# State products of a chunked gated recurrence: three products of 32 columns per head become one of 96

## The chip, the cores and the metric

The kernel runs on one core of a Trainium2 chip. The engines that matter are TensorE (PE; its weight loads are shown apart as PEld), VectorE (DVE), ScalarE (ACT), GpSimd (POOL) and SyncE (SP), which issues the DMAs. The metric is the time of one execution on the device in microseconds, as the median of the runs. PE multiplies a stationary operand (`lhsT`, the "weights", at most 128 rows by 128 columns) with a moving one (`rhs`) and writes to PSUM. A weight load and the pass that streams the moving operand are two instructions in the trace. An fp32 product shows as two loads and two passes, a transpose as one of each.

## The reference

A gated linear recurrence with complex decay, for each batch (4), head (8) and channel (48) over 768 steps, and behind it a feed-forward block on 3072 tokens:

```python
for t in range(S):
    new_re = ar * S_re - ai * S_im
    new_im = ar * S_im + ai * S_re
    kv = np.einsum('bhd,bhe->bhde', k[:, :, t], v[:, :, t])
    S_re, S_im = (new_re + kv, new_im)
    y[:, :, t] = np.einsum('bhd,bhde->bhe', q[:, :, t], S_re)
...
a = x @ w1
b = x @ w2
h = a * b @ w3
return (h @ w_out).astype(np.float32)
```

`ar` and `ai` are the gates after their magnitude is limited to 0.999; `x` is `y` with the heads laid side by side (3072 by 384); the hidden width is 1024.

## The kernel before

A batch's 768 steps are cut into two units of 384, so there are 8 units, and each unit into three chunks of 128 steps. `gates(u)` works out the running product of the gates (logarithms, exponentials, scans, sine and cosine, on ACT and DVE) and scales and turns q and k with it. In that scaled frame the decay disappears: the output of a step is a masked sum over earlier steps of its chunk plus q times a state that only grows by sums. `move` brings q and k by DMA into tiles `QL` and `KL` of 96 rows (real and imaginary parts of 48 channels) per head. At a unit's end the state is scaled once with `rho`.

For each chunk PE does four kinds of work.

- `turn(u, c, x)` (L677) transposes the chunk's scaled k, three blocks of 128x128 for each of the real and imaginary part, into a PSUM bank `tp`; ACT copies it to `KT` (L679), which then has 128 steps in its rows and 96 columns beside each other per head.
- `state(u, c)` (L742) multiplies `KT` of a head with that head's v (128 steps by 48) into a bank `kv` of 96 rows by 8 heads by 48. The columns of `KT` go in three groups of 32, one product each, into rows 0 to 31, 32 to 63 and 64 to 95 of the bank. DVE then adds `kv` to the state `T` (L748), or ACT copies it where there is no state yet (L746).
- `scores(u, c, x)` (L691) forms the products of q and k in blocks of 32 keys into the banks `sc`; DVE copies them through a causal mask into `A` (L694).
- `outputs(u, c)` (L725) forms `y` from `A` and v and from `T` and `QL`; ACT copies it to `xT` (L727).

The feed-forward work of unit u-1 fills PE between these pieces of unit u: `ffn_ab` (m, L766: products with w1 and w2, then ACT's copy `a`, L771, and DVE's product `ab`, L772), and the output products (o, L853; p, L817) with `w3o`, a product of the two last weight matrices that is formed at the start (f, L995).

The state update runs 20 times: three times in a batch's first unit, twice in its second, whose last state nobody reads. `pieces(u)` lists the pieces of a unit in order and `unit` puts feed-forward work between them; behind `kv` come m, p, sc or, in the first units, tp. The order on PE is the program's own (`manual_schedule`). On ACT, DVE, POOL and SP a planner sets the order, by its own times and by marks of priority such as those on the add into `T`. `tp`, `kv` and `y` share the two banks of the pool `ps_v`.

In the trace's names a form such as 128*32 is the number of rows and columns of the stationary operand that are in use.

Of the kernel before, what the change touches and what calls it, by code (L numbers as in the profile page):

```python
# [375 lines left out]
def kernel(  # L376
# [36 lines left out]
    nc = tc.nc  # L413
    B, H, D, S = qt.shape
# [18 lines left out]
    SB, LANES = 32, C // 32  # L433
# [83 lines left out]
    def load_v(u):  # L517
        b, h = divmod(u, 2)


        vr = one.tile([P, UC, DM], FP, tag="vr", name="vr")
        nc.sync.dma_start(out=vr, in_=v[b, h * TT:(h + 1) * TT].rearrange("(c p) e -> p c e", p=C))
        g_t[u]["vr"] = vr
# [209 lines left out]
    def state(u, c):  # L733

        KT, V = KT_t.pop((u, c)), g_t[u]["vr"][:, c].rearrange("p (h d) -> p h d", d=D)
        n = u % 2 * UC + c
        T = T_t.get((u // 2, n))
        kv = ps_v.tile([2 * D, H, D], FP, tag="v", name="kv")
        for hd in range(H):
            rows = KT[:, hd].rearrange("p d x f -> p (d x f)")  # L740
            for g in range(0, 2 * D, SB):
                nc.tensor.matmul(out=kv[g:g + SB, hd], lhsT=rows[:, g:g + SB], rhs=V[:, hd], start=True, stop=True)  # L742
        Tn = Tb[(u * UC + c) % 3]
        with tc.high_priority():
            if T is None:
                nc.scalar.copy(out=Tn[:, :, 0:D], in_=kv)  # L746
            else:
                add = nc.vector.tensor_tensor(out=Tn[:, :, 0:D], in0=kv, in1=T[:, :, 0:D], op=OP.add)  # L748
                if (u, c) == (0, 1):

                    tc.add_manual_dep(add.ins, begun[-1].ins.name, ORDER, reason="begun")
        if c == UC - 1:
            rho = L_t[u][1][:, :, TT:TT + 1].to_broadcast([2 * D, H, D])
            nc.vector.tensor_tensor(out=Tn[:, :, 0:D], in0=Tn[:, :, 0:D], in1=rho, op=OP.mult)
        T_t[u // 2, n + 1] = Tn
        if u + 1 < NU and c == UC - 1 - u % 2:
            load_v(u + 1)
# [269 lines left out]
    def pieces(u):  # L1027

        sc = [[lambda c=c, x=x: scores(u, c, x) for x in range(2)] for c in range(UC)]
        tr = [[lambda c=c, x=x: turn(u, c, x) for x in range(2)] for c in range(UC)]  # L1030
        kv = [lambda c=c: state(u, c) for c in range(UC)]
        y = [lambda c=c: outputs(u, c) for c in range(UC)]

        if u % 2:
            return [[tr[0][0]], [tr[0][1]], [tr[1][0], kv[0]], [tr[1][1]], [kv[1]], sc[0], sc[1] + [y[0]], sc[2] + [y[1]],
                    [y[2]]]
        return [[tr[0][0]], [tr[0][1]], [tr[1][0], kv[0]], [tr[1][1]], [tr[2][0], kv[1]], [tr[2][1]], [kv[2]] + sc[0],
                sc[1] + [y[0]], sc[2] + [y[1]], [y[2]]]
# [144 lines left out]
```

## Time and profile before

| | |
|---|---|
| median of 3 runs | 560.96 us (560.75 to 561.29) |
| the profiled execution | 561.29 us, span 559.5 us |
| mean granted clock of PE | 0.988 |
| PE busy | 525.5 us, 5474 passes |
| DVE, ACT busy | 334.8 us, 338.0 us |
| L742, passes of kv | 960, 206 ns each by the trace's modelled ends, side by side |
| L742, weight loads of kv | 960, 110 ns each |
| L748, DVE's add into T | 16, 554 ns each |
| L746, ACT's copy into T | 4, 475 ns each |
| kv's share of the chain that ended last | 2% |

Passes on PE overlap, and their recorded ends are modelled, so lengths of single passes can't be added up: what a group costs is read from the start of its first pass to the start of what follows. A group of the profile counts both passes of a product: 20 states x 8 heads x 3 groups x 2 = 960.

### The profile page before, as it was taken

The page shows a single profiled execution, that of the slowest core. Times are in us where ns is not written, and L with a number is a line of the kernel's source. Part 1 is how long each engine was busy: PE and PEld are TensorE (multiplying, and loading weights), DVE is VectorE, ACT ScalarE, POOL GpSimd, SP SyncE. Part 2 cuts the span into 40 slices and gives each one's busy share as a digit, 9 for nine tenths or more (in the row PEclk, how much of TensorE's full clock was granted, in tenths as well). Part 3 has the DMA queues.
Part 4 walks back from the last instruction along what each step waited for, and adds up shares of the span by engine and source line. Part 5 has one row for each costly group of instructions (what it writes and reads, how often), then busy time and mean ns, then how long its engine had stood idle before and what let it go on. Part 6 is the DMA issues. An engine that isn't in the chain of part 4 may idle for free.

```text
span 559.5 us, 13023 instructions
## 1 busy us (share of the span) xinstructions
PE 525.5 (94%) x5474; PEld 359.1 (64%) x5474; DVE 334.8 (60%) x516; ACT 338.0 (60%) x553; POOL 5.2 (1%) x12
## 2 busy tenths in 40 slices
PE   4698789999999999999999999999999999999995
PEld 2354565567656875569656875687557965696564
DVE  8999398936862457536852677446752797332121
ACT  6989665735564688738782898569964845201100
POOL 3000000000000000000000000000000000000000
PEclk9999989999999999999999999999999999999998
DMA  8997988794556557875685565956674204300001
GB/s 254 349 403 175 276 217 262 205 190 139 114 152 131 136 161 203 206 208 152 178 213 159 174 146 164 242 162 184 170 184 135 74 29 95 80 13 30 0 1 49
DMA packets 73156, 89.71 MB, mean 160 GB/s; under 512 B 31104, under 2 KB 62848, under 8 KB 72320
## 3 DMA queue, kind: packets, MB, share of 16 engines
q1 hardware_dynamic: 73088, 88.79, 58.0%
q8 instruction: 45, 0.74, 0.6%
q14 instruction: 23, 0.19, 0.1%
HBM read 65.14 MB, written 4.72 MB: 125 GB/s over the span
## 4 chain that ended last, share of the span: by engine, by line
PE 53%; DVE 18%; ACT 16%; issue 5%; DMA 4%; SPq 2%; DVEq 0%; ACTq 0%
PE m L766 26%; PE o L853 8%; PE p L817 7%; PE y L725 4%; PE sc L691 4%; ACT gZ L562 3%; ACT re L562 3%; DVE gA L598 3%; DVE gZ L621 2%; PE kv L742 2%; ACT gR L562 2%; PE tp L677 2%; ACT gA L562 2%; ACT low L899 1%; DVE gR L640 1%
## 5 line engine op out<-in xcount | busy, mean ns | idle before, releaser
L766 PE MATMUL m<-xT,w1s 128*128 128x384 f32 x384 | 135.3, 489 | 1.8 <-ACT xT L727 1.8
L766 PE MATMUL m<-xT,w2s 128*128 128x384 f32 x384 | 134.5, 487 | 0.3 <-DVE ab L772 0.3
L766 PEld LDWEIGHTS m<-xT,w2s 128*128 128x128 f32 x384 | 72.8, 190 | 51.8 <-DVE ab L772 1.5
L766 PEld LDWEIGHTS m<-xT,w1s 128*128 128x128 f32 x384 | 71.1, 190 | 47.4 <-ACT xT L727 2.4
L772 DVE TENSOR_TENSOR ab<-m,a 128x384 f32<-128x384 f32 x64 | 35.3, 553 | 81.0 <-PE m L766 74.8
L771 ACT COPY a<-m 128x384 f32<-128x384 f32 x64 | 30.3, 475 | 53.9 <-PE m L766 52.7
L853 PE MATMUL o<-w3o,ab 128*128 128x384 f32 x160 | 54.0, 487 | 0.0
L679 ACT COPY KT<-tp 128x384 f32<-128x384 f32 x40 | 33.7, 853 | 31.1 <-PE tp L677 30.9
L694 DVE COPY_PREDICATED A<-mask,sc 128x512 f32<-128x512 uint8 x48 | 33.2, 730 | 14.6 <-PE sc L691 14.4
L853 PEld LDWEIGHTS o<-w3o,ab 128*128 128x128 f32 x160 | 29.6, 190 | 18.7 <-issue 0.4
L725 PE MATMUL y<-A,V 128*32 128x128 f32 x768 | 40.8, 279 | 0.0
L691 PE MATMUL sc<-QL,KL 96*32 96x64 f32 (+3 forms) x1536 | 33.8, 238 | 6.6 <-DVE A L694 3.0
L691 PEld LDWEIGHTS sc<-QL,KL 96*32 96x32 f32 x1536 | 29.1, 112 | 13.0 <-issue 5.1
L725 PE MATMUL y<-QL,T 96*32 96x128 f32 x640 | 36.6, 280 | 0.4 <-issue 0.4
L995 PE MATMUL f<-wo_s,w3s 128*128 128x384 f32 x96 | 36.6, 528 | 0.0
L725 PEld LDWEIGHTS y<-A,V 128*32 128x32 f32 x768 | 34.7, 112 | 1.4 <-issue 1.4
L748 DVE TENSOR_TENSOR T<-kv,T 96x384 f32<-96x384 f32 x16 | 8.8, 553 | 43.6 <-PE kv L742 43.4
L899 ACT ACTIVATE low<-raw 128x384 uint16<-128x384 uint32 (+4 forms) x28 | 24.9, 900 | 14.0 <-DVE low L895 7.3
L725 PEld LDWEIGHTS y<-QL,T 96*32 96x32 f32 x640 | 32.6, 113 | 0.9 <-issue 0.9
L817 PE MATMUL p<-To,So 128*128 128x192 f32 x168 | 31.6, 335 | 0.0
L995 PEld LDWEIGHTS f<-wo_s,w3s 128*128 128x128 f32 x96 | 20.0, 212 | 14.3 <-issue 4.5
L817 PEld LDWEIGHTS p<-To,So 128*128 128x128 f32 x168 | 27.0, 190 | 3.2 <-issue 3.0
(119 smaller groups left out, 738.8 us busy)
## 6 DMA issues: line engine op xcount, KB each, us to landing
look<-in_w_dram SPq DMA_DIRECT2D x28, 512.0 KB, 4.4
raw<-in_w_dram SPq DMA_DIRECT2D x6, 1024.0 KB, 10.6
raw<-in_w_dram SPq DMA_DIRECT2D x8, 768.0 KB, 9.2
KL<-gR SPq DMA_DIRECT2D x24, 192.5 KB, 3.2
KL<-k SPq DMA_DIRECT2D x24, 192.5 KB, 4.0
re<-in_a_re_dram SPq DMA_DIRECT2D x24, 192.0 KB, 5.7
im<-in_a_im_dram SPq DMA_DIRECT2D x24, 192.0 KB, 3.9
k<-in_k_dram SPq DMA_DIRECT2D x24, 192.0 KB, 4.6
```

The costliest lines, as they stand in the source:

```text
L562: chain(nc.scalar.activation(**kw))
L679: nc.scalar.copy(out=KT_t[u, c][:, :, :, x].rearrange("p h d f -> p f d h"), in_=tp.rearrange("p f (d h) -> p f d h", h=H))
L691: nc.tensor.matmul(out=sc[SB * g:SB * g + SB, j, s0:C], lhsT=KL[:, x * n + j, w][:, s0:s0 + SB], rhs=QL[:, x * n + j, w][:, s0:C], start=T ...
L694: masked[:] = [nc.vector.copy_predicated(out=A[:, x * n:(x + 1) * n], data=sc, mask=mask)]
L725: nc.tensor.matmul(out=o, lhsT=a, rhs=b, start=s0, stop=s1)
L766: nc.tensor.matmul(out=m, lhsT=w[:, j * P // WB, f, j * P % WB:j * P % WB + P], rhs=xT_t[u][:, f], start=(f == 0), stop=(f == KD - 1))
L771: copied[:] = [nc.scalar.copy(out=a, in_=got[0])]
L772: nc.vector.tensor_tensor(out=ab_t[u][:, j], in0=got[1], in1=a, op=OP.mult)
L817: nc.tensor.matmul(out=m[p], lhsT=a[:, f], rhs=b[:, f], start=(f == 0), stop=(f == KH - 1))
L853: nc.tensor.matmul(out=m, lhsT=ab_t[u][:, f, t * P:(t + 1) * P], rhs=w3o[:, f], start=(f == 0), stop=(f == KF - 1))
L899: nc.scalar.activation(out=ends.bitcast(U16)[:, 0::2].rearrange("p (r m) -> p r m", r=r), in_=lo.bitcast(U32), func=AF.Copy, scale=2.0 ** -29)
L995: nc.tensor.matmul(out=sums[j], lhsT=w3_t[f][:, j * P:(j + 1) * P], rhs=w3_t["wo"][:, f], start=(f == 0), stop=(f == KF - 1))
```

## The change

In `state`, the three products of 32 columns per head are replaced with one product of all 96 columns. It reads the same `KT` and v and writes the same place in the same bank; there are 8 products per state instead of 24.

```diff
         kv = ps_v.tile([2 * D, H, D], FP, tag="v", name="kv")
         for hd in range(H):
-            rows = KT[:, hd].rearrange("p d x f -> p (d x f)")
-            for g in range(0, 2 * D, SB):
-                nc.tensor.matmul(out=kv[g:g + SB, hd], lhsT=rows[:, g:g + SB], rhs=V[:, hd], start=True, stop=True)
+            nc.tensor.matmul(out=kv[:, hd], lhsT=KT[:, hd].rearrange("p d x f -> p (d x f)"), rhs=V[:, hd],
+                             start=True, stop=True)
         Tn = Tb[(u * UC + c) % 3]
```

Nothing else differs: pools, order of the pieces, loads and stores are the same.

## The prediction

> **What bounds the kernel now.** I read the page first: the line of TensorE's (PE) busy time, its row in the 40 slices, and the chain of work that ended last. Then, from the trace, PE's waits after the start-up, the timeline and the chain around one state update, and the groups of the tiles that are neighbours of it.
>
> ```profile
> PE 525.5 (94%) x5474; PEld 359.1 (64%) x5474; DVE 334.8 (60%) x516; ACT 338.0 (60%) x553; POOL 5.2 (1%) x12
> ...
> PE   4698789999999999999999999999999999999995
> ...
> PE 53%; DVE 18%; ACT 16%; issue 5%; DMA 4%; SPq 2%; DVEq 0%; ACTq 0%
> ```
>
> PE is busy in every slice after the first seven (some 100 us). A busy matmul row is not yet a bound, so the waits decide; this is all that PE waited for from 80 us on:
>
> ```profile
> PE tp L677 <- DVE gR L640: 3.1, 4, 1.3
> PE m L766 <- ACT xT L727: 1.8, 2, 1.1
> PE sc L691 <- issue: 1.4, 3, 0.8
> PE y L725 <- issue: 0.4, 1, 0.4
> PE m L766 <- DVE ab L772: 0.3, 1, 0.3
> PE sc L691 <- DVE A L694: 0.3, 1, 0.3
> PE tp L677 <- ACT KT L679: 0.2, 1, 0.2
> ```
>
> Some 7.5 us in 480 us. The reader should see that what PE issues there sets the pace, and that nothing in the list is a wait of or for kv. One state update in the timeline of PE and its weight loads (start, length, engine, line):
>
> ```profile
> 173.93 0.49 PE L677 MATMUL tp<-ident,gR 128*128 128x128 f32 x3
> ...
> 174.35 0.75 PEld L742 LDWEIGHTS kv<-vr,KT 128*32 128x32 f32 x48 [0.17 <-issue]
> 174.35 0.88 PE L742 MATMUL kv<-vr,KT 128*32 128x48 f32 x48
> ...
> 175.16 1.59 PEld L766 LDWEIGHTS m<-xT,w1s 128*128 128x128 f32 x6
> 175.16 2.20 PE L766 MATMUL m<-xT,w1s 128*128 128x384 f32 x6
> ```
>
> and the chain in the same place, where the whole burst lies on it:
>
> ```profile
> 174.09 0.33 PE tp L677 x3
> 174.42 0.81 PE kv L742 x48
> 175.23 2.78 PE m L766 x8
> ```
>
> Asked at each of the 20 bursts, the chain holds such a piece of 0.81 at 15 of them, all from 174 us on: six followed by m, six by p, three by sc (at 188.98, 310.24 and 431.75). The three at 58, 62 and 64 us lie under a DMA, ACT and DVE chain, and the two of the second unit, at 121.89 and 126.01, under DMAs. Now the durations in ns (least, median, most):
>
> ```profile
> L742 PEld LDWEIGHTS kv<-vr,KT x960: 106/110/110, 58.4 to 488.5; 128*32 128x32 f32 x192
> L742 PE MATMUL kv<-vr,KT x960: 206/206/231, 58.4 to 488.6; 128*32 128x48 f32 x192
> ...
> L766 PE MATMUL m<-xT,w1s x384: 486/486/590, 84.7 to 536.9; 128*128 128x384 f32 x192
> ...
> L677 PE MATMUL tp<-ident,k x60: 272/273/329, 56.3 to 482.5; 128*128 128x128 f32 x60
> ...
> 175.16 0.30 PEld L766 LDWEIGHTS m<-xT,w1s 128*128 128x128 f32 x2
> ```
>
> The most is each time a first pass behind a change of form, which waits in the open for its weights: 25 ns for kv's 32 columns, 104 for m's 128, 57 for a transpose's 128. The last line, a narrow window, has m's first two loads, 0.19 long each, in 0.30: the second starts 108 ns after the first. So a load for products takes 0.83 ns per column. A stream takes as much: m's six passes start 1.93 us apart, 322 ns per 384 columns; 48 columns come to 40 ns and 2.5 for the pass.
>
> **The change part by part.** *Removed:* per state 24 products of 32 columns, recorded as 48 loads and 48 passes (two per fp32 product). *Added:* 8 products of 96 columns, 16 loads and 16 passes. Values, banks and releases stay.
>
> What a burst costs before, from the end of the last transpose's stream (173.93 + 3 x 0.11 = 174.26) to the place where m streams: a gap of 95 ns to kv's first start; the burst of 16 rounds, three passes beside each other 6 ns apart, rounds 42.5 ns apart, whose last starts 675 ns after the first; 40 ns of stream; a gap of 96; 104 for m's bare load. Sum 1011 ns (the three column groups run truly beside each other, or 48 passes would need 2 us). The gap is that of a change of form: all neighbours of one form in this trace follow at 2 to 3 ns (tp to m, m to o), all changes between 128*128 and 128*32 at 93 to 97.
>
> After it, the passes are of 128 rows and 96 columns. I take them for the neighbours' form, since 96 doesn't fit one 32-column group, so that the two changes go, and the first load, 80 ns, fits beside the last transpose's 107 ns. But each pass needs its own 96 columns: 96 x 0.83 + 1.7 = 81.7 ns, under a stream of only 42.5 ns. m's timeline shows that one load goes ahead and the next starts as its pass starts, so the period is the longer of the two. Then: 15 x 81.7 = 1225 to the last pass's start, and 108 for m's load, which starts with it: 1333 ns. That is **+0.32 us** where m or p follows, twelve times: +3.9 us.
>
> Where sc follows, today's 990, 993 and 1030 ns from the previous stream's end to sc's start become 1225 + 40 + 96 (p to sc, as in 15 other places) + 25 for the bare load = 1386: +0.40, +0.39, +0.36, **+1.15 us** in all. Today's gap there is 180, not 96, since four semaphore instructions of 110 ns each stand in PE's queue behind 96 short ones; behind 32 in a longer time they are early, which is counted in that.
>
> The two bursts of the second unit and the three of the start I cost at nothing: behind them PE waits for KT's copy, or for sc (0.25 to 2.3 us in those places), and the chain is a DMA's or the gates'. If that cover failed they would add up to 5 x 0.4 = 2.0 us. The add into T (DVE, 0.55 us) and the copy into T (ACT, 0.48) start later by the growth; their readers, y of a later chunk and the next state, come over 2 us later, and ps_v's bank is asked for again only behind a product of 2 us. On ACT and DVE those two stand ahead of other work that is queued in order; it gets later as PE does, no more. DMA, SP and POOL issue nothing different, besides 1280 fewer PE instructions to fetch.
>
> Does PE's lateness reach the end? At the last burst of each unit the chain goes on in PE and passes from there to ACT or DVE (PE y at 193.95, ACT xT at 194.90, then the gates until PE's wait at 227.17). So the gates are started by PE, and the 3.1 us that PE waits for them don't swallow it.
>
> Sum: 3.9 + 1.15 = +5.0 us. The profiled execution took 561.29 (span 559.5 and 1.8 around it), so 566.3; it is 0.33 above the median of the three, so the median to expect is **566.0**.
>
> The unknown is a load of 96 columns, which no row has. Bounds: it costs as a transpose's does, 57 x 96/128 = 43 ns, and then the stream sets 42.5 to 43: a burst is 15 x 42.5 + 108 = 745, -0.27 x 12, and 798 to sc, -0.20 x 3, **-3.8 us**. Above, it takes the time of 128 columns, 108: 1728, +0.72 x 12, and 1781, +0.78 x 3, **+10.9**. Or 96 columns are a form of their own, with both gaps and both bare loads: 95 + 80 + 1225 + 40 + 95 + 108 = 1643, +0.63 x 12, and +0.56 x 3, **+9.3**. I take 81.7, as 32 and 128 columns of these same two-pass products lie on one line.
>
> The Trainium skill, "TensorE: Matmul & The Clock Gate", section "Part 3: Packing small matmuls — row/col tiling", says that a weight load overlaps a running matmul only where the row groups differ. By that rule a pass here would cost load and stream, 124 ns, and a sum worked out from it would be some +16 us (577). The row speaks against it: m's passes use all 128 rows and still follow at 322 ns, the stream alone.
>
> **The rivals.** *Loads hidden, faster:* the load is no longer than the stream. For it: the transposes' 57 ns per 128 columns. Against: those are one-pass transposes, and m's and p's first passes pay 104. It decides where a pass takes under 60 ns (15 x 60 + 108 = 1008); its time is 560.96 - 3.8 = 557.2. *Dearer loads or a form of its own:* for it, that 96 is in no row; against, the line through 25 and 104. 570.3 to 571.9. *Swallowed by waits:* PE's waits for gR and xT, 4.9 us, shrink by what kv grows: 561 to 563. Against it, the chain comes from PE behind every burst. *Planner:* ACT, DVE and SP are put in order by a planner that works with its own times, and 640 fewer passes may turn neighbours there. One gate step moved past a copy is worth about an operation of 1.2 to 1.4 us per unit, either way: 562 to 570.
>
> **How the numbers follow.** The forecast's case has 0.70 (564.5 to 567.5), hidden loads 0.09, dearer ones 0.08, swallowed 0.04, planner 0.09. Leaving out hidden loads, the part of the swallowed below 562.5 and the dearest gives 562.5 to 570.5, and some 0.85 inside. Faster by over 0.2% (about what a measurement here tells from none): 0.09 and some of the planner's, 0.11; within: 0.03; slower: 0.86.
>
> **What would show it.** Right: 320 passes of kv, starting some 82 ns apart, a burst of about 1.3 us in the chain, no 95 ns gap on either side, and m's first pass recorded 42 ns behind kv's last, some 552 ns long (486 and what its load outlasts kv's stream) instead of 590. Wrong: passes 42 ns apart, gaps of 95 that stay, or PE's waits for gR shrinking by what the bursts grow.

## The result and the profile after

The changed kernel takes 566.66 us (median of 4 runs, 565.88 to 567.67) where the kernel before took 561.12 beside it: a ratio of 1.0097, 95% interval 1.0075 to 1.0119. It is slower by 5.5 us; 566.0 was forecast, with 562.5 to 570.5 as the range.

The page of the changed kernel: PE's line, its chain, and the new group of state products.

```profile
PE 532.0 (94%) x4834; PEld 369.8 (65%) x4834; DVE 334.5 (59%) x516; ACT 337.6 (60%) x553; POOL 5.3 (1%) x12
...
PE 61%; ACT 15%; DVE 14%; DMA 4%; issue 4%; SPq 1%; DVEq 0%; ACTq 0%
PE m L765 27%; PE o L852 9%; PE p L816 9%; PE y L725 5%; PE kv L740 4%; PE sc L691 4%; ACT re L562 3%; DVE gZ L621 3%; PE tp L677 2%; ACT gZ L562 2%; DVE gA L598 2%; DMA look<-in_w_dram 2%; ACT gR L562 2%; ACT gA L562 1%; DVE gR L640 1%
...
L740 PE MATMUL kv<-vr,KT 128*96 128x48 f32 x320 | 29.7, 246 | 1.1 <-ACT KT L679 1.1
```

PE has 640 passes fewer and is busy 6.5 us longer. kv's share of the chain went from 2% to 4%. The rest of the program is as before: DVE and ACT do the same work in the same time.

The timeline of PE and its loads around the state update that the prediction showed (start, length):

```profile
173.53 0.49 PE L677 MATMUL tp<-ident,gR 128*128 128x128 f32 x3
...
173.75 1.46 PEld L740 LDWEIGHTS kv<-vr,KT 128*96 128x96 f32 x16
...
173.85 1.48 PE L740 MATMUL kv<-vr,KT 128*96 128x48 f32 x16
...
175.13 1.59 PEld L765 LDWEIGHTS m<-xT,w1s 128*128 128x128 f32 x6
175.17 2.17 PE L765 MATMUL m<-xT,w1s 128*128 128x384 f32 x6
```

The first load starts at 173.75, under the last transpose, and the first pass directly behind that transpose (173.53 + 3 x 0.11 = 173.86): the gap of 95 ns is gone on both sides. But from the first stream at 173.85 to the moment m's load can begin, at 175.13, the 16 passes take 1.275 us, 15 periods of 85.0 ns. The chain in the same place:

```profile
173.69 0.33 PE tp L677 x3
174.02 1.32 PE kv L740 x16
175.33 2.97 PE m L765 x9
```

The piece that was 0.81 us of 48 passes is 1.32 of 16. And PE's waits from 80 us on:

```profile
PE tp L677 <- DVE gR L640: 3.1, 4, 1.4
PE m L765 <- ACT xT L727: 1.8, 2, 1.0
PE y L725 <- issue: 1.1, 1, 1.1
PE m L765 <- DVE ab L771: 1.0, 2, 0.8
PE m L765 <- ACT a L770: 0.4, 1, 0.4
PE sc L691 <- DVE A L694: 0.3, 1, 0.3
```

The waits for gR and for xT are what they were (3.1 and 1.8 us): they swallowed nothing. The waits called "issue" went from 1.8 to 1.1 us, those for ab and a from 0.3 to 1.4.

With each of PE's other 4514 passes set against its twin in the trace of before, the lateness is -0.4 us ahead of the first burst of the third unit, grows by 0.38 to 0.42 at each of the fifteen bursts from there on, and is +5.2 at the last product. Between the bursts it moves too, and that nearly evens out: +0.8 us between the bursts at 246 and 296 us, where PE now waits 1.0 us for ab instead of 0.3, and -1.2 between those at 310 and 357, most of it where the waits "issue" at 315.0 and 319.8 are gone. The span has grown by 6.4; the other 1.2 us lies behind the last DVE add (5.5 us before, 6.7 after), and with times of 565.9 to 567.7 in four runs I don't lay it to the change.

### The profile page after: what moved, and what is told of

Same layout as the page of the kernel before. It is cut to its first block, busy times and chain, and to the rows that moved or that the text cites. A ratio compares the mean times of both kernels' runs of the same rounds, so it can differ in the third digit from the quotient of the medians.

```text
span 565.9 us, 11743 instructions
## 1 busy us (share of the span) xinstructions
PE 532.0 (94%) x4834; PEld 369.8 (65%) x4834; DVE 334.5 (59%) x516; ACT 337.6 (60%) x553; POOL 5.3 (1%) x12
## 4 chain that ended last, share of the span: by engine, by line
PE 61%; ACT 15%; DVE 14%; DMA 4%; issue 4%; SPq 1%; DVEq 0%; ACTq 0%
PE m L765 27%; PE o L852 9%; PE p L816 9%; PE y L725 5%; PE kv L740 4%; PE sc L691 4%; ACT re L562 3%; DVE gZ L621 3%; PE tp L677 2%; ACT gZ L562 2%; DVE gA L598 2%; DMA look<-in_w_dram 2%; ACT gR L562 2%; ACT gA L562 1%; DVE gR L640 1%
## 5 line engine op out<-in xcount | busy, mean ns | idle before, releaser
L725 PE MATMUL y<-A,V 128*32 128x128 f32 x768 | 39.0, 273 | 0.0
L725 PE MATMUL y<-QL,T 96*32 96x128 f32 x640 | 34.9, 272 | 1.1 <-issue 1.1
L725 PEld LDWEIGHTS y<-A,V 128*32 128x32 f32 x768 | 33.4, 109 | 1.4 <-issue 1.4
L725 PEld LDWEIGHTS y<-QL,T 96*32 96x32 f32 x640 | 31.4, 109 | 1.4 <-issue 1.4
L740 PEld LDWEIGHTS kv<-vr,KT 128*96 128x96 f32 x320 | 29.6, 165 | 2.5 <-ACT KT L679 1.3
L740 PE MATMUL kv<-vr,KT 128*96 128x48 f32 x320 | 29.7, 246 | 1.1 <-ACT KT L679 1.1
```

Source lines behind the costliest of these rows:

```text
L725: nc.tensor.matmul(out=o, lhsT=a, rhs=b, start=s0, stop=s1)
L740: nc.tensor.matmul(out=kv[:, hd], lhsT=KT[:, hd].rearrange("p d x f -> p (d x f)"), rhs=V[:, hd], start=True, stop=True)
```

## The experiments

**Does the load or the stream set the pace?** First, the changed kernel with twice the stream. The second half of what a product writes is written over by the next head's own.

```diff
-            nc.tensor.matmul(out=kv[:, hd], lhsT=KT[:, hd].rearrange("p d x f -> p (d x f)"), rhs=V[:, hd],
+            n2 = min(hd + 2, H)
+            nc.tensor.matmul(out=kv[:, hd:n2], lhsT=KT[:, hd].rearrange("p d x f -> p (d x f)"), rhs=V[:, hd:n2],
```

> The changed kernel, but each product streams the v of two heads (96 columns instead of 48; the second half is written over by the next head's own product, the last head keeps 48). Theory (the load of 96 columns sets the pace, one load ahead): a pass is 85.0 ns in the trace of the changed kernel, the longer stream is 80 + 2.5 = 82.5 ns and fits under it, so passes stay 85 ns apart and the time stays 566.7 us (565.5 to 568). Rival (load and stream of a pass come one after another, since all use the same rows): 14 of 16 passes grow by 40 ns, 0.56 us per state, 15 states on the chain: +8.4, 575 us.

Measured: 568.06 us, ratio to the kernel before 1.0103 (1.0074 to 1.0132), where the changed kernel has 1.0097. The group of kv in its trace, and a burst:

```profile
L741 PE MATMUL kv<-vr,KT x320: 208/248/323, 59.1 to 494.1; 128*96 128x96 f32 x140, 128*96 128x48 f32 x20
...
174.81 1.46 PEld L741 LDWEIGHTS kv<-vr,KT 128*96 128x96 f32 x16
...
174.92 1.48 PE L741 MATMUL kv<-vr,KT 128*96 128x96 f32 x16
...
176.19 1.59 PEld L766 LDWEIGHTS m<-xT,w1s 128*128 128x128 f32 x6
```

From the first stream to m's load it is 1.27 us, as without the longer stream. Twice the streamed columns cost nothing: the load sets the pace, and load and stream of different passes do overlap though both use all 128 rows. The Trainium skill's rule in "TensorE: Matmul & The Clock Gate", section "Part 3: Packing small matmuls — row/col tiling", that loads overlap running matmuls only where the row groups differ, doesn't hold by itself here: by it this kernel would have lost some 8 us more (an estimate, 14 x 40 ns on 15 states). The same section also lets a load go ahead into a background weight buffer, and passes that stay 85 ns apart agree with that.

The same lengthening in the kernel before:

> The kernel before with its three column groups, streaming 96 columns of v instead of 48 in the same way. Theory (there the stream sets the pace, the 32-column load of 28 ns is under it): 14 of 16 rounds go from 42.5 to 82.5 ns, +0.56 us per state on 15 states: +8.4, 569.5 us (568 to 571). Rival (a round is three loads or issues one after another, 3 x 14 ns): 561 to 563 us.

Measured: 568.9 us, ratio 1.012 (1.0093 to 1.0147), +7.2 us against 561.72 beside it.

```profile
174.31 1.30 PEld L743 LDWEIGHTS kv<-vr,KT 128*32 128x32 f32 x48 [0.17 <-issue]
174.31 1.44 PE L743 MATMUL kv<-vr,KT 128*32 128x96 f32 x48
...
175.68 1.26 PEld L767 LDWEIGHTS m<-xT,w1s 128*128 128x128 f32 x5
```

The burst goes from 0.81 to 1.37 us: here the stream sets the pace, and loads of 32 columns are hidden. So the change moved the state update from the one regime to the other. The +7.2 us are less than the 8.4 forecast, since the three bursts in front of sc grow by only 0.3 us each (12 x 0.56 + 3 x 0.3 = 7.6). There sc starts 6 ns behind a pass of kv and ahead of the burst's last three:

```profile
190.06 1.40 PE L743 MATMUL kv<-vr,KT 128*32 128x96 f32 x45
191.26 0.30 PE L691 MATMUL sc<-QL,KL 96*32 96x128 f32 x1
191.28 0.22 PE L743 MATMUL kv<-vr,KT 128*32 128x48 f32 x3
```

So kv in groups of 32 columns and sc, with 96 rows and 32 columns, are of one form: no gap lies between them.

**How the pace goes by the columns loaded.** A product that loads 128 columns, 32 of the next head's beside its own (`rows` now runs over the columns of all heads, and the bank `kv` has 128 rows):

```diff
-            nc.tensor.matmul(out=kv[:, hd], lhsT=KT[:, hd].rearrange("p d x f -> p (d x f)"), rhs=V[:, hd],
+            n = P if hd + 1 < H else 2 * D
+            nc.tensor.matmul(out=kv[0:n, hd], lhsT=rows[:, 2 * D * hd:2 * D * hd + n], rhs=V[:, hd],
```

> The changed kernel, but a product loads 128 columns (96 of its head and 32 of the next one, whose rows 96 to 127 of the result nobody reads; the last head keeps 96). Theory (the pace goes by the columns loaded): passes 112 ns apart instead of 85, 14 per state: +0.38 us on 15 states, +5.7, 572.4 us (571 to 574). Rival (a fixed cost per full-width pass, whatever its columns): 566.7 us.

Measured: 573.83 us, ratio 1.021 (1.0181 to 1.0239); 5.8 us more than the run with the longer stream, which shared the chip with it. And one that loads only 64:

```diff
-            nc.tensor.matmul(out=kv[:, hd], lhsT=KT[:, hd].rearrange("p d x f -> p (d x f)"), rhs=V[:, hd],
+            nc.tensor.matmul(out=kv[0:64, hd], lhsT=KT[:, hd].rearrange("p d x f -> p (d x f)")[:, 0:64], rhs=V[:, hd],
```

> The changed kernel, but a product loads the first 64 columns alone and DVE and ACT add or copy 64 rows; the last 32 rows of the state are left out and stay zero. Theory (pace by columns loaded): 64 x 0.83 + 3 to 5 = 56 to 58 ns per pass, -27 x 16 = -0.43 us per state, -6.5 on 15: 560.2 us if 64 columns are no form of their own, and 560.2 + 15 x 0.3 = 564.7 if the gaps of 95 ns and the bare loads come back. Rival (a fixed cost per pass): 566.7 us.

Measured: 565.53 us, ratio 1.0054 (1.003 to 1.0077). First the burst with 128 columns, then that with 64:

```profile
239.82 1.83 PE L742 MATMUL kv<-vr,KT 128*128 128x48 f32 x16
...
241.45 1.59 PEld L767 LDWEIGHTS m<-xT,w1s 128*128 128x128 f32 x6
```

```profile
236.66 0.49 PE L677 MATMUL tp<-ident,gR 128*128 128x128 f32 x3
...
237.09 1.13 PE L740 MATMUL kv<-vr,KT 128*64 128x48 f32 x16
...
238.15 1.59 PEld L765 LDWEIGHTS m<-xT,w1s 128*128 128x128 f32 x6
238.15 2.20 PE L765 MATMUL m<-xT,w1s 128*128 128x384 f32 x6
```

The starts of successive loads lie 58, 85 and 112 ns apart for 64, 96 and 128 columns: a line of 0.83 ns per column and some 5 ns per load. But with 64 columns the gaps came back: the last transpose ends at 236.99 and kv starts 95 ns behind it, and m's group is 2.20 long, as before the change, not 2.17, since its load lies bare again. So 64 columns are a form of their own and 96 are not, which is the case that the prediction took without a row for it.

**Does PE's lateness reach the end?** The changed kernel with every state product made twice:

```diff
-        for hd in range(H):
+        for hd in [*range(H), *range(H)]:
```

> The changed kernel with every state product made twice, the second over the first. Theory (PE sets the pace and passes its lateness on): 16 passes x 85 ns = 1.36 us per state, 15 states on the chain: +20.4, 587 us (584 to 592). Rival (PE's waits for gR and xT, 4.9 us, and those of the second unit swallow what a burst grows): 582 us or less.

Measured: 591.28 us, ratio 1.0527 (1.0498 to 1.0556), 24.6 us above the changed kernel. Pass against pass, its trace is later by 1.36 us more at each burst but the third, the two of the second unit among them. The three of the very first unit leave 0.9 us of lateness ahead of the second. From there it grows to 23.4 us at the last product, by 22.5, where 17 bursts make 23.1 and 15 would make 20.4. So it is 17 bursts that count, not the 15 that lay on the chain: that the two of the second unit stood beside waits of PE was no cover. PE's waits in this trace:

```profile
PE tp L677 <- DVE gR L640: 3.2, 4, 1.3
PE y L725 <- issue: 2.8, 2, 1.6
PE m L765 <- ACT xT L727: 1.8, 2, 1.0
...
PE m L765 <- DVE ab L771: 0.2, 1, 0.2
```

The waits for gR and xT, which the rival named, have not shrunk. Those for ab and a have, from 1.4 to 0.2 us, but those called "issue" have grown by 1.7, about as much.

**What the two changes of form were worth.** If 296 ns of a burst before the change are changes of form and a bare load, then moving bursts together should give that back. In the kernel before, the bursts moved beside the first scores:

```diff
-            return [[tr[0][0]], [tr[0][1]], [tr[1][0], kv[0]], [tr[1][1]], [kv[1]], sc[0], sc[1] + [y[0]], sc[2] + [y[1]],
+            return [[tr[0][0]], [tr[0][1]], [tr[1][0]], [tr[1][1]], [], kv[0:2] + sc[0], sc[1] + [y[0]], sc[2] + [y[1]],
...
-        return [[tr[0][0]], [tr[0][1]], [tr[1][0], kv[0]], [tr[1][1]], [tr[2][0], kv[1]], [tr[2][1]], [kv[2]] + sc[0],
+        return [[tr[0][0]], [tr[0][1]], [tr[1][0], kv[0]], [tr[1][1]], [tr[2][0]], [tr[2][1]], kv[1:3] + sc[0],
```

(The very first unit keeps its order here and in the others that follow.)

> The kernel before (three column groups), with the state bursts moved in the order of the pieces: in each batch's second unit both directly ahead of the first scores, in its first unit (but for the very first) the second burst beside the third. Theory (of the 1011 ns of a burst among 128*128 work, 296 are two changes of form and the bare load): 0.296 us less in three units and 0.41 less in three or four (there the change from p to sc goes too): -2.1 to -2.5, 558.7 us (558 to 559.5). Rival (the moved bursts make new waits, on KT, on the bank or on T): 561 us or more.

Measured: 561.72 us, ratio 1.0014 (0.9992 to 1.0036): no gain. PE's waits in its trace, the first four lines:

```profile
PE tp L677 <- DVE gR L640: 3.0, 3, 1.3
PE y L725 <- issue: 2.5, 4, 1.0
PE sc L691 <- issue: 2.0, 4, 1.0
PE m L766 <- ACT xT L727: 1.0, 1, 1.0
```

The bursts did get shorter (two of them take 1.36 us from first to last pass, with no gap between), but the waits "issue", in sc, y and p, went from 1.8 to 4.8 us and ate it. The rival named KT, the bank or T; it was none of these.

The same move in the changed kernel:

> The changed kernel with the bursts moved in the same way. Theory (its products are of the neighbours' form, so there are no changes to save, only m's or p's bare load beyond kv's stream, 70 ns each): 0.07 x 3 + 0.14 x 4 = -0.8, 565.9 us (565 to 567). Rival (the place of a burst is worth the same in both kernels): -2.3, 564.4 us.

Measured: 564.9 us, ratio 1.0063 (1.0038 to 1.0089), about 1.9 us better than the changed kernel in its usual order, by ratios whose intervals overlap. That lies between the two values. Its trace has waits "issue" of 0.7 us and 0.8 instead of 1.8 for xT, and m's wait of 1.0 us for ab is gone, so part of it is waits that happened to close; how much of it belongs to the place of the bursts is not settled.

Is it the density of short instructions that makes PE wait for "issue"? To test that, the kernel with the bursts beside the scores, without the third column group, which changes the number of instructions and not the length of a burst:

```diff
-            for g in range(0, 2 * D, SB):
+            for g in range(0, 64, SB):
```

> The kernel before with the bursts beside the scores, and without the third column group: the last 32 rows of the state are left out and stay zero. Rounds run side by side, so a burst takes the same 0.68 us with a third fewer instructions. Theory (the bursts beside the scores lost 3.0 us to PE waiting for its own instructions, since short ones stand too close): that wait, 4.8 us with three groups, falls to 2 or 3, and the time by as much, 559 to 560. Rival (the loss is a wait on KT, the bank or T, which two groups need as much): 561.7 as with three groups.

> The kernel before in its own order, without the third column group (the last 32 rows of the state are left out): the control for that. A burst keeps its 16 rounds of 42.5 ns and its two changes of form. Theory: only the wait for instructions, 1.8 us here, can fall, so -0.5 to -1.5: 560.3 to 561.3. Rival (a round takes as long as its loads one after another): a third off 0.68 us, 17 times: -3.9, 558.

Measured: 558.79 us, ratio 0.9962 (0.9927 to 0.9998), for the moved bursts, and 562.74, ratio 1.0014 (0.9995 to 1.0034), for the control. The waits of the two, one line each:

```profile
PE o L853 <- issue: 0.9, 1, 0.9
PE sc L691 <- issue: 0.8, 2, 0.4
```

```profile
PE y L725 <- issue: 3.4, 2, 2.2
PE sc L691 <- issue: 0.5, 1, 0.5
```

The first is as the theory had it: 4.8 falls to 1.7 us, and the time by 2.9. The control goes against it: with a third fewer state instructions in the old order the wait rose from 1.8 to 3.9 us. So the loss of the moved bursts goes with this wait, but "fewer instructions, less wait" is not a rule. In both runs sc also starts 60 ns behind kv's last pass instead of 220 and more: with a third fewer instructions of kv in the same time, the four semaphore instructions in front of sc no longer hold it up. That is 0.16 us a place or more, which the list of waits hides, since the recorded ends of kv's passes cover most of it. The control did show that a burst of 32 passes is as long as one of 48 (669 and 675 ns from first to last pass): the groups run side by side.

Where the waits "issue" stand can be read from the traces. Count what PE has issued before such a wait: a load and a pass each time, and the semaphore instructions between them. For all 35 of them after 70 us, in the traces of all twelve kernels, the number is 192 or 193 beyond a multiple of 256. Each ends 1.2 to 1.6 us after the end of a packet of 16384 bytes on the DMA queue whose kind the profile gives as "instruction"; of the kernel before:

```profile
q8 instruction: 45, 0.74, 0.6%
```

Its 11026 instructions on PE are 43 blocks of 256; the changed kernel has 9746, 38 blocks, and 40 packets. So PE waits there, by all signs, for its next block of instructions. Short instructions are needed for it: of 446 blocks in the twelve traces, the 273 that took PE over 5.4 us (the wait not counted) end without one, and all 35 waits are among the other 173. They are not enough, as 138 of these end without a wait too. A change in the number of instructions moves the ends of the blocks to other work, so the wait can grow with fewer of them. No run moved the ends of the blocks alone, so what decides within the short ones stays open.

The moved bursts together, but away from the scores, in the kernel before:

```diff
-            return [[tr[0][0]], [tr[0][1]], [tr[1][0], kv[0]], [tr[1][1]], [kv[1]], sc[0], sc[1] + [y[0]], sc[2] + [y[1]],
+            return [[tr[0][0]], [tr[0][1]], [tr[1][0]], [tr[1][1]], kv[0:2], sc[0], sc[1] + [y[0]], sc[2] + [y[1]],
...
-        return [[tr[0][0]], [tr[0][1]], [tr[1][0], kv[0]], [tr[1][1]], [tr[2][0], kv[1]], [tr[2][1]], [kv[2]] + sc[0],
+        return [[tr[0][0]], [tr[0][1]], [tr[1][0]], [tr[1][1]], kv[0:2] + [tr[2][0]], [tr[2][1]], [kv[2]] + sc[0],
```

> The kernel before (three column groups), with the first two bursts of each unit but the very first made directly behind each other, one piece after the second chunk's transposes, and away from the first scores. Theory (a pair saves two changes of form and a bare load, 296 ns, and PE's wait for its own instructions, which grew where the bursts stood beside the scores, does not grow here): 7 x 0.296 = -2.1, 559.7 us against some 561.8 of the kernel before on the same chips (558.8 to 560.6). Rival (a pair of 192 short instructions is as dense as the bursts beside the scores): 561 to 562.

Measured: 558.69 us against 561.63 beside it, ratio 0.9962 (0.9942 to 0.9982): 2.1 us by the ratio, and faster than both kernels. Two bursts in its trace, and PE's waits "issue", unchanged at 1.8 us:

```profile
182.59 1.56 PE L742 MATMUL kv<-vr,KT 128*32 128x48 f32 x96
184.09 0.55 PE L677 MATMUL tp<-ident,gR 128*128 128x128 f32 x3
...
PE sc L691 <- issue: 1.3, 2, 0.7
PE y L725 <- issue: 0.5, 1, 0.5
```

96 passes in one piece, with one change of form ahead and one behind.

## Why the prediction was right, point by point

- *PE sets the pace and passes its lateness on.* Right, and shown by the doubled products. The count was off: 17 bursts pass their growth on, not 15. The two of the second unit had been costed at nothing for the waits beside them; the bound of 0.4 us each for a failed cover was fair. In the change itself they add 0.13 and 0.42 us at their places, but that doesn't show in the end, since waits "issue" behind them closed: before, PE waits 0.92 us inside sc at 130.41 and 0.59 inside y at 140.02 (from the end of the stream; the list of waits, which goes by recorded ends, has 0.8 and 0.4), and after the change it doesn't. Lateness ahead of the third unit is -0.4 us in the two traces, in which those bursts' growth is contained.
- *A pass goes by its load.* Right, and shown by the longer stream. The size was a little low: 85.0 ns, not 81.7, since a load that sets the pace has some 5 ns of its own, not the 1.7 read from m's two loads; and m's load behind it takes 112 ns, not 108. A burst in front of m or p so costs 15 x 85.0 + 112 = 1387 ns instead of the 1333 forecast, +0.38 and not +0.32. Of the signs that the prediction named, m's first pass is 555 ns long (552 forecast), but it is recorded 85 ns behind kv's last and not 42.
- *96 columns are of the neighbours' form.* Right: gaps of 2 to 3 ns ahead of kv, none of 95. The 64-column run shows what it would have cost otherwise.
- *kv in front of sc.* From the previous stream's end to sc's start it is 1413 ns and 27 for the bare load, where 1386 was forecast; the same 85 ns. The growth is +0.42, +0.42 and +0.38, which the lateness of sc shows: the bare load counts on neither side, since before the change three of sc's first four passes wait for theirs too. One reading was wrong, at no cost to the sum: today's gap of 180 ns was set against the 96 of a change of form, but between kv in column groups and sc there is none, as the longer stream showed, and nearly the whole of the 180 is the wait behind the four semaphore instructions (18 ns are left with two column groups). After the change they are hidden, as forecast: the gap behind kv's last record is 138 ns, the change of form (96) and the last pass's wait for its own load (42).
- *The sum.* From the third unit on: 12 x 0.38 + 0.42 + 0.42 + 0.38 = 5.8 us, less the 0.4 of the first two units and some 0.1 to 0.2 of waits, which is the 5.2 us of lateness at the last product. The medians differ by 5.5, with 4.2 to 6.7 as the interval of the ratio. That the 5.0 forecast came so near is in part luck: the period was too short by 0.8 us in all, and the waits, which the prediction left as they were, moved by about 1 us both ways and nearly cancelled.
- *The rivals.* Hidden loads (faster) needed a pass under 60 ns; it takes 85. Dearer loads took 112 ns only with 128 columns in fact loaded. The waits for gR and xT swallowed nothing. The planner turned nothing: the 553 instructions of ACT, 516 of DVE, 12 of POOL and 408 DMA issues of SP come in the same order in both traces.

## What to carry to other kernels

Where a product has a short moving operand, compare load and stream before merging: the period of back-to-back passes is the longer of the two, here 0.83 ns for each column loaded and about as much for each column streamed, so 96 loaded against 48 streamed loses, although it is one third of the instructions. Column groups beside each other hide their loads, but each visit from work of another form costs two gaps of 95 ns and a bare load, so put such visits together; in this kernel that was worth 2.1 us in one order of the pieces (1.0 to 3.3 by the interval), and nothing in another, where the waits "issue" grew as much. Merging the groups into wide products cost 5.5.

## What was not expected

Twice the streamed columns were free (48 to 96, at 85 ns per pass). And PE's waits for "issue", which the list of waits puts down to nothing, differ between 0.2 and 4.8 us from one kernel to the next with the same products around them, nearly as much as the change itself moved. They all stand at one place in PE's blocks of 256 instructions, so a change in the number of instructions can move the time by itself.
